# Attention and two mixture-of-experts layers in one kernel: small attention matmuls of two tiles in joined runs, weight splits on VectorE only, five residual-row buffers

## The chip, the cores and the metric

The kernel runs on one core of one Trainium2 chip. The metric is the device time of one execution in microseconds (us), as a median of several runs. The core has five engines with a queue of instructions each, which they work off in order: TensorE (PE, matmuls; its weight loads are listed apart as PEld), VectorE (DVE), ScalarE (ACT), GpSimd (POOL) and SyncE (SP, which here only issues DMAs). Engines wait for each other by semaphores.

## What is computed

```python
# q, k, v: (8, 8, 576, 64); attention inside chunks of 64 positions
scores = q_c @ k_c.T / sqrt(64); attn = softmax(scores); out = attn @ v_c
x = out.transpose(0, 2, 1, 3).reshape(4608, 512)
# layer 1, dense: w_in (512, 2048), w_out (2048, 512)
x = (s * relu(x @ w_in) ** 2 + b) @ w_out
# layer 2: 8 experts, w1[e] (512, 1024), w2[e] (1024, 512)
do = x @ w_skip > 0                       # other rows pass unchanged
e = argmax(x[do] @ w_gate); gate = softmax(x[do] @ w_gate)[e]
out[do] = x[do] + gate * (relu(x[do] @ w1[e]) @ w2[e])
```

All of it is float32. A product is made of three passes of a faster format: each operand is split into a high part (rounded) and a low part (the rest), and high x low, low x high and high x high are summed in PSUM.

## The kernel before

The 4608 rows are 36 tiles of 128 rows, in 13 chunks of 2, 3, 2, then nine times 3, then 2 tiles. Per tile `t` the attention is a chain over the engines: `att_sc` (TensorE, 16 matmuls of 64x64, line 230) writes the scores into PSUM, `att_max` and `att_sub` (VectorE), `att_exp` (ScalarE), `att_sum` (VectorE), `att_norm` (GpSimd or VectorE, line 255), `att_tr` (four transposes on TensorE, line 263), `att_cp` (ScalarE), `att_pv` (TensorE, 16 matmuls of 64x64, line 278), `att_hi` and `att_lo` (ScalarE, VectorE), which split the result into `xh` and `xl`. Queries and keys of one tile have one buffer (`qk`), the values one (`v`); the scores have the PSUM bank `sc`, the outputs `po`.

Per chunk `c` the dense layer takes 16 steps `f`: `p1_mm` (line 306, 12 matmuls into `ph`), `p1_sq` (ScalarE, lines 313 and 314) and `p1_g` (VectorE, lines 330 to 333), then `p2` (line 349, three matmuls per tile of the chunk into the `acc` banks). After step 15 `evac` (ScalarE, line 361) copies each tile's sum from PSUM into a residual-row buffer `x1` of the pool `op_`; from there it goes to `out` (line 364), its router logits are made (line 369 on VectorE, or lines 377 to 392 by way of TensorE), and after the routing (`route_a`, `route_b`, lines 409 to 462) the row, with its gate, is written to `x1s` in HBM (line 439). Only when that write has landed is the `x1` buffer free again. The pool has three such buffers. Chunk 1 accumulates in the banks `acc2`, `sc` and `tp`, so the scores of tile 7 need the copies of chunk 1 to be over. The last chunk copies two tiles. The weights of the dense layer are turned from int64 words into float32 and split in the first 130 us, and each conversion (`conv_scale`) holds an `x1` buffer too.

The second layer works on items: an expert's weights and up to 256 gathered rows. An item has 8 steps `mm1` (line 677, 12 matmuls) and 8 steps `mm2` (line 695, 6 matmuls). The expert's weights land as float32 in `whr` and `wlr` and are split into `win_h` (`split_hi`, ScalarE, line 636) and `win_l` (`split_lo`, line 639); step `f` of `mm1` needs split `f`, of `mm2` split `8 + f`. Items 0 and 1 are picked before the last chunk is routed; items 2 and on come from tables made of the counts (`tables_n`, `tables_b`, `table`), need the rows gathered by GpSimd (line 628), and run in a chain of branches at the end.

The order on all engines up to item 2 comes from `Plan`, a list scheduler in the kernel: `add` gives each operation its engine (or two to choose from), a cost, what it follows, an urgency, and rings of buffers that it takes and frees. `run` always puts the operation next that could start first, by those costs. So a changed ring or cost moves instructions everywhere.

Of the kernel before, what the change touches and what calls it, by code (L numbers as in the profile page):

```python
# [24 lines left out]
NTILE = NT // P  # L25
# [14 lines left out]
class Plan:  # L40
# [75 lines left out]
def fused_kernel(ctx: ExitStack, tc: tile.TileContext, qk, v, w_in, w_out, sb, wl, wlp, w1, w2,  # L116
# [6 lines left out]
    def pool(name, bufs=1, **kw):  # L123
        return ctx.enter_context(tc.tile_pool(name=name, bufs=bufs, **kw))
# [9 lines left out]
    ep = pool("ep", 2)  # L134
    qp = pool("qp")
    gp = pool("gp", 3)
    op_ = pool("op", 3)
    rp = pool("rp")
    ps = pool("ps", space=PSUM)
    ps_h = pool("ps_h", 2, space=PSUM)  # L140
# [148 lines left out]
    def att_hi(t):  # L289
        S.activation(out=xcols(t)[0], in_=po_t[t], func=AF.Copy)  # L290
# [63 lines left out]
    lg = {}  # L354
# [142 lines left out]
    r2 = {}  # L497
# [308 lines left out]
    with tc.manual_schedule():  # L806
# [29 lines left out]
                T.matmul(pro["pw"], zw[:, :P], zw, start=True, stop=True)  # L836

        rings = {n: 1 for n in ("acc0", "acc1", "acc2", "sc", "tp", "po", "qk", "v")}
        rings.update({"e": 2, "et": 2, "x1": 3, "ph": 2, "g": 3, "lg": 2, "xhl": 2, "r2": 3, "o": 2, "r": 2})
        fill(11)  # L840
        pl = Plan(rings, fill, "a0_0", {"DMA": 1.7, "PE": 5.8})
        add = pl.add
# [24 lines left out]
        def entry(t):  # L867
# [3 lines left out]
                return HURRY + t  # L871
            return 8 + 4 * (t - 5) if c == 2 else N0 + (c - 3) * NF + 5 * (t - T0[c])


        tags = {0: ("sc", "tp", "po"), 1: ("acc0", "acc1", "acc2"), 2: ("sc", "tp", "po"), 3: ("acc0", "acc1", "acc2"),
                4: ("sc", "tp", "po"), 5: ("po", "po", "po"), 6: ("po", "po", "po")}
# [4 lines left out]
            last[tag] = f"{done}{t}"  # L881
        for t in range(NTILE):
            for n in ("sc", "tr", "pv", "sub", "cp", "hi"):
                turn.setdefault(f"{n}{t}", []).extend([f"{n}{t - 1}"] if t else [])
        for t in range(NTILE):
            c = chunk_of[t]
            x, y, z = tags.get(t, ("sc", "tp", "po"))
            i = entry(t)
            h = i if t < 3 else i + HURRY / 2
            if t >= 5:  # L890
                add(f"ld_qk{t}", "DMA", 1.46, lambda t=t: load_qk(t), [f"ld_qk{t - 1 if t > 5 else 0}"], max(i - 8, 20 + 2 * (t - 5)), take=["qk"])
                add(f"ld_v{t}", "DMA", .73, lambda t=t: load_v(t), [f"ld_v{t - 1 if t > 5 else 0}"], max(i - 7, 21 + 2 * (t - 5)), take=["v"])
            w = [f"ev1_{j}" for j in range(3)] if t == 7 else []
            own = t == 0 or t >= 5
            add(f"sc{t}", "PE", 1.9 if t == 0 else 1.3, lambda t=t, x=x: att_sc(t, x), [f"ld_qk{t}"] + w + turn[f"sc{t}"], i,
                [x], [("qk", f"ld_qk{t}")] if own else [])
            add(f"mx{t}", "DVE", .6, lambda t=t: att_max(t), [f"sc{t}"], h)
            add(f"sub{t}", "DVE", .6, lambda t=t: att_sub(t), [f"mx{t}"] + turn[f"sub{t}"], h, ["e"], [(x, f"sc{t}")])
# [8 lines left out]
            add(f"pv{t}", "PE", 1.3, lambda t=t, z=z: att_pv(t, z), [f"cp{t}", f"ld_v{t}"] + turn[f"pv{t}"], i + 2, [z],  # L907
                [("et", f"cp{t}")] + ([("v", f"ld_v{t}")] if own else []))
            first = t == T0[c]
            add(f"hi{t}", "ACT", .48, lambda t=t: att_hi(t), [f"pv{t}"] + ([] if first else [f"hi{T0[c]}"]), h,  # L910
                ["xhl"] if first else [])
            add(f"lo{t}", "DVE", .6, lambda t=t: att_lo(t), [f"hi{t}"], h, [], [(z, f"pv{t}")])


        for u in range(2 * NF):
# [206 lines left out]
        for m in range(3):  # L1122
            i = iE + 20 * (m - 1)
            for u in range(16):
                if m == 0:
                    w = [f"a{L}_{u}"]
                else:
                    w = [f"m{m - 1}_{u}" if u < 8 else f"n{m - 1}_{u - 8}"]
                ld_ = f"s_w{m}{u // 8}" if m < 2 else f"t_w0{u // 8}"
                p = i + 4 + u  # L1130
                rw = (lambda m: r2["raw"][m % 2])
                add(f"sh{m}_{u}", "ACT", .52, lambda m=m, u=u: split_hi(r2["raw"][m % 2], u), [ld_] + w + ([f"sh{m}_{u - 1}"] if u else []), p)
                add(f"sl{m}_{u}", ("DVE", "POOL"), (.6, 1.23), lambda eng, m=m, u=u: split_lo(r2["raw"][m % 2], u, eng), [f"sh{m}_{u}"], p)
# [107 lines left out]
```

## Time and profile before

| | us |
|---|---|
| three runs | 1362.92, 1360.46, 1362.91; median 1362.91 |
| the profiled execution, its own time | 1361.95 |
| its span, first to last instruction | 1359.8 |
| PE busy in the span | 1301.1 (96%) |
| DVE busy | 987.0 (73%) |
| ACT busy | 571.7 (42%) |
| POOL busy | 199.5 (15%) |

All times in the rows are counted from the span's start. Matmul durations overlap: a 128x384 matmul is shown with 0.33 us and the next one starts 0.17 us later, so the distance of starts is what it costs. "x32" merges consecutive records; an instruction "x16" of the program shows as 32 records here. In brackets stands how long the engine had been idle and for whom it waited. Line numbers are those of the kernel before; up to line 836 the changed kernel has the same.

### The profile page before, as it was taken

The page shows a single profiled execution, that of the slowest core. Times are in us where ns is not written, and L with a number is a line of the kernel's source. Part 1 is how long each engine was busy: PE and PEld are TensorE (multiplying, and loading weights), DVE is VectorE, ACT ScalarE, POOL GpSimd, SP SyncE. Part 2 cuts the span into 40 slices and gives each one's busy share as a digit, 9 for nine tenths or more (in the row PEclk, how much of TensorE's full clock was granted, in tenths as well). Part 3 has the DMA queues.
Part 4 walks back from the last instruction along what each step waited for, and adds up shares of the span by engine and source line. Part 5 has one row for each costly group of instructions (what it writes and reads, how often), then busy time and mean ns, then how long its engine had stood idle before and what let it go on. Part 6 is the DMA issues. An engine that isn't in the chain of part 4 may idle for free. (4 is left out here: it accounts for less than half of the span.)

```text
span 1359.8 us, 23872 instructions
## 1 busy us (share of the span) xinstructions
PE 1301.1 (96%) x9107; PEld 1154.8 (85%) x9110; DVE 987.0 (73%) x2322; ACT 571.7 (42%) x1131; POOL 199.5 (15%) x210
## 2 busy tenths in 40 slices
PE   7899999999999999999999999999679999999896
PEld 5788888898888888888888888899668989999774
DVE  7896477649486775859486776847778888878674
ACT  4797433232232323232232333232526555656463
POOL 0000001000101010100101010101644212121243
PEclk9999989999999999999999999999889999999998
DMA  6553214111212132141213131112839656566473
GB/s 250 180 183 128 63 53 92 46 52 43 48 63 56 47 36 83 25 85 32 48 63 56 50 49 67 16 34 79 257 106 401 257 206 228 211 234 211 172 285 123
DMA packets 43019, 160.46 MB, mean 118 GB/s; under 512 B 11370, under 2 KB 11754, under 8 KB 38142
## 3 DMA queue, kind: packets, MB, share of 16 engines
q1 hardware_dynamic: 36526, 142.55, 33.6%
q0 software_dynamic: 6352, 16.12, 3.4%
q8 instruction: 78, 1.28, 0.4%
q14 instruction: 63, 0.52, 0.1%
HBM read 132.68 MB, written 27.20 MB: 118 GB/s over the span
## 5 line engine op out<-in xcount | busy, mean ns | idle before, releaser
L313 ACT ACTIVATE r<-ph 128x384 f32<-128x384 f32 (+1 forms) x208 | 96.5, 464 | 441.9 <-PE ph L306 433.0
L306 PE MATMUL ph<-xh,win_l 128*128 128x384 f32 (+1 forms) x832 | 274.9, 330 | 2.8 <-DVE win_l L206 1.4
L306 PE MATMUL ph<-xl,win_h 128*128 128x384 f32 (+1 forms) x832 | 269.6, 324 | 1.4 <-DVE xl L294 1.4
L306 PE MATMUL ph<-xh,win_h 128*128 128x384 f32 (+1 forms) x832 | 269.9, 324 | 0.0
L349 PE MATMUL acc<-wout_h,gl 128*128 128x512 f32 x544 | 220.4, 405 | 3.7 <-DVE gl L333 3.7
L349 PE MATMUL acc<-wout_l,gh 128*128 128x512 f32 x544 | 214.4, 394 | 0.0
L349 PE MATMUL acc<-wout_h,gh 128*128 128x512 f32 x544 | 213.0, 392 | 0.0
L330 DVE TENSOR_SCALAR r<-r,sb_sb 128x384 f32<-128x384 f32 (+1 forms) x176 | 84.8, 482 | 172.6 <-ACT r L314 166.9
L369 DVE CUSTOM_DVE_ANT_0 junk<-x,wl_sb 128x512 bf16<-128x512 f32 x270 | 191.3, 708 | 6.1 <-ACT x L361 0.4
L306 PEld LDWEIGHTS ph<-xh,win_l 128*128 128x128 f32 x832 | 156.5, 188 | 11.3 <-DVE win_l L206 2.1
L306 PEld LDWEIGHTS ph<-xl,win_h 128*128 128x128 f32 x832 | 156.6, 188 | 7.4 <-DVE xl L294 1.6
L695 PE MATMUL ac<-win_h,hhl 128*128 128x512 f32 x480 | 156.0, 398 | 1.1 <-DVE hhl L776 1.0
L306 PEld LDWEIGHTS ph<-xh,win_h 128*128 128x128 f32 x832 | 156.5, 188 | 0.0
L333 DVE TENSOR_TENSOR gl<-r,gh 128x384 fp32r<-128x384 f32 (+1 forms) x208 | 109.6, 527 | 30.2 <-ACT gh L320 24.1
L639 DVE TENSOR_TENSOR win_l<-wlr,win_h 128x512 fp32r<-128x512 f32 x121 | 98.4, 832 | 35.4 <-ACT win_h L636 35.3
L677 PE MATMUL ph<-xh,win_l 128*128 128x256 f32 x416 | 118.8, 286 | 3.8 <-ACT r L683 3.0
L349 PEld LDWEIGHTS acc<-wout_h,gh 128*128 128x128 f32 x544 | 102.4, 188 | 23.2
L349 PEld LDWEIGHTS acc<-wout_h,gl 128*128 128x128 f32 x544 | 102.5, 188 | 22.8 <-DVE gl L333 3.9
L677 PE MATMUL ph<-xl,win_h 128*128 128x256 f32 x416 | 118.3, 284 | 0.5 <-DVE xl L655 0.5
L677 PE MATMUL ph<-xh,win_h 128*128 128x256 f32 x416 | 118.2, 284 | 0.0
L349 PEld LDWEIGHTS acc<-wout_l,gh 128*128 128x128 f32 x544 | 102.8, 189 | 13.8
L695 PEld LDWEIGHTS ac<-win_h,hhl 128*128 128x128 f32 x480 | 91.4, 190 | 21.3 <-DVE hhl L776 2.7
(227 smaller groups left out, 2072.7 us busy)
## 6 DMA issues: line engine op xcount, KB each, us to landing
whr<-in_w SPq DMA_DIRECT2D x18, 2048.0 KB, 7.8
wlr<-in_w SPq DMA_DIRECT2D x18, 2048.0 KB, 10.8
qk<-in_qk SPq DMA_DIRECT2D x32, 512.0 KB, 10.0
x1s<-x SPq DMA_DIRECT2D x36, 264.0 KB, 9.1
out<-x SPq DMA_DIRECT2D x36, 256.0 KB, 2.3
v<-in_v SPq DMA_DIRECT2D x32, 256.0 KB, 2.7
stg<-in_w_in SPq DMA_DIRECT2D x16, 512.0 KB, 3.3
stg<-in_w_out SPq DMA_DIRECT2D x16, 512.0 KB, 3.3
```

The source lines that it names most:

```text
L306: T.matmul(ph, a[:, f, k * P:(k + 1) * P], b[c][:, k, :n], start=(i == 0), stop=(i == 11))
L313: S.activation(out=r, in_=ph_t.pop((c, f)), func=AF.Relu)
L330: V.tensor_scalar(out=r, in0=r, scalar1=sb_sb[:, 0:1], scalar2=sb_sb[:, 1:2], op0=ALU.mult, op1=ALU.add)
L333: V.tensor_tensor(out=gl, in0=r, in1=b32(gh), op=ALU.subtract)
L349: T.matmul(acc[c][j], a[:, j * P:(j + 1) * P], wo(b, f), start=(f == 0 and n == 0), stop=(f == NF - 1 and n == 2))
L369: V.tensor_tensor_reduce(out=junk, in0=x1t[T0[c] + j][:, :D], in1=wl_sb[0][:, i, :], op0=ALU.mult, op1=ALU.add, scale=1.0, scalar=0.0, acc ...
L639: ENG[eng].tensor_tensor(out=win_l[:, u, :], in0=raw[u // 8][:, u % 8, :], in1=b32(win_h)[:, u, :], op=ALU.subtract)
L677: T.matmul(ph, w[:, f, j * P:(j + 1) * P], r2[x][:, j, :], start=(n == 0), stop=(n == 11))
L695: T.matmul(ac[t], r2[h][:, f, t * P:(t + 1) * P], w[:, 8 + f, :], start=(f == 0 and n == 0), stop=(f == 7 and n == 2))
```

## The change

There are three edits.

The residual-row buffers `x1` go from three to five, in the pool and in the scheduler's ring.

For tiles 8 to 34 `att_pv(t)` and `att_sc(t + 1)` are one operation of the scheduler, `ps{t}`, so that the 64x64 matmuls of the two stand directly behind each other on TensorE. It follows all that the two followed. The scores of tile `t + 1` are so made earlier than before.

The splits `sl0`, `sl1` and `sl2` (the low parts of the weights of the items 0, 1 and 2) may no longer go to GpSimd.

```diff
-    op_ = pool("op", 3)
+    op_ = pool("op", 5)
...
-        rings.update({"e": 2, "et": 2, "x1": 3, "ph": 2, ...
+        rings.update({"e": 2, "et": 2, "x1": 5, "ph": 2, ...
...
+        JOIN = range(8, NTILE - 1)
+
+        def att_join(t):
+
+            att_pv(t, "po")
+            att_sc(t + 1, "sc")
...
+            if t - 1 not in JOIN:
+                add(f"sc{t}", "PE", 1.9 if t == 0 else 1.3, lambda t=t, x=x: att_sc(t, x), ...
...
+            if t in JOIN:
+                add(f"ps{t}", "PE", 2.2, lambda t=t: att_join(t),
+                    [f"cp{t}", f"ld_v{t}", f"ld_qk{t + 1}"] + turn[f"pv{t}"] + turn[f"sc{t + 1}"], i + 2, ["po", "sc"],
+                    [("et", f"cp{t}"), ("v", f"ld_v{t}"), ("qk", f"ld_qk{t + 1}")])
...
-                add(f"sl{m}_{u}", ("DVE", "POOL"), (.6, 1.23), lambda eng, m=m, u=u: split_lo(r2["raw"][m % 2], u, eng), [f"sh{m}_{u}"], p)
+                add(f"sl{m}_{u}", "DVE", .6, lambda m=m, u=u: split_lo(r2["raw"][m % 2], u, "DVE"), [f"sh{m}_{u}"], p)
```

What this does to the order shows at three places. The first is TensorE in a middle chunk, around the `att_pv` of one tile (`po`), first before:

```order
L306 MATMUL ph<-xl,win_h 128x384
L306 MATMUL ph<-xh,win_h 128x384
L278 MATMUL po<-et,v 64x64 x16
L349 MATMUL acc_3345<-wout_h_102,gl 128x512
L349 MATMUL acc_3345<-wout_l_103,gh 128x512
```

And now:

```order
L306 MATMUL ph<-xl,win_h 128x384
L306 MATMUL ph<-xh,win_h 128x384
L278 MATMUL po<-et,v 64x64 x16
L230 MATMUL sc<-qk 64x64 x16
L349 MATMUL acc_3345<-wout_h_102,gl 128x512
L349 MATMUL acc_3345<-wout_l_103,gh 128x512
```

The scores of the next tile, which stood by themselves some four large steps later, follow at once. In the order before, two of the 27 pairs already stood like this (tiles 8 and 9, and 9 and 10).

The second place is ScalarE at the end of chunk 1, whose three tiles are copied out of `acc`, `sc` and `tp`, first before:

```order
L313 ACTIVATE r<-ph 128x256
L314 ACTIVATE r<-r 128x256
L361 ACTIVATE x_1856<-acc_630 128x512
L313 ACTIVATE r<-ph 128x256
L314 ACTIVATE r<-r 128x256
L361 ACTIVATE x_1890<-sc 128x512
L361 ACTIVATE x_1897<-tp 128x512
```

And now:

```order
L313 ACTIVATE r<-ph 128x256
L314 ACTIVATE r<-r 128x256
L361 ACTIVATE x_1856<-acc_659 128x512
L361 ACTIVATE x_1858<-sc 128x512
L361 ACTIVATE x_1863<-tp 128x512
L313 ACTIVATE r<-ph 128x256
```

The three copies are made in a row. On TensorE the scores of tile 7 (`sc7`) move up one large step, to right behind the first `p2` of chunk 2.

The third place is VectorE after the last large step of the dense layer, from the split of item 0's rows (`xl`) on, first before:

```order
L655 TENSOR_TENSOR xl_9823<-tp2a,xh_9822 128x4x128
L655 TENSOR_TENSOR xl_9823<-tp2b,xh_9822 128x4x128
L639 TENSOR_TENSOR win_l<-whr_9810,win_h 128x512 x3
L688 CAST hhl<-r_9879 128x256
L689 TENSOR_TENSOR hhl<-r_9879,hhl 128x256
L392 COPY lg<-pl 128x9
```

And now:

```order
L655 TENSOR_TENSOR xl_9823<-tp2a,xh_9822 128x4x128
L655 TENSOR_TENSOR xl_9823<-tp2b,xh_9822 128x4x128
L392 COPY lg<-pl 128x9 x2
L409 TENSOR_REDUCE m<-lg 128x2
L410 TENSOR_TENSOR key<-lg,m 128x16
L411 TENSOR_TENSOR key<-key,cst_sb 128x16
```

The routing of the last chunk now stands ahead of item 0's splits; on TensorE its logits and counts likewise stand ahead of item 0's first `mm1`, where before they stood among its steps. And GpSimd, in the same stretch, had before:

```order
L639 TENSOR_TENSOR win_l<-whr_9810,win_h 128x512 x5
L436 MEMSET x_9863 128x15
L436 MEMSET x_9867 128x15
L639 TENSOR_TENSOR win_l<-wlr_9811,win_h 128x512 x2
L467 DMA idl<-ids_sb,si 37120x1 x2
L639 TENSOR_TENSOR win_l<-wlr_9811,win_h 128x512 x3
L639 TENSOR_TENSOR win_l<-whr_10055,win_h 128x512 x6
L708 DMA out<-et,idxs_9632 4608x512
```

And has now:

```order
L467 DMA idl<-ids_sb,si 37120x1 x2
L436 MEMSET x_9858 128x15
L436 MEMSET x_9860 128x15
L708 DMA out<-et,idxs_9632 4608x512 x2
L628 DMA xg_10264<-x1s,idx_9944 128x528 x2
```

24 splits of the items 0 to 2 leave GpSimd; VectorE has 48 of them instead of 24.

## Rows read from the trace of the kernel before

**Rows 1.** Waits of PE in the whole span: us in total, times, longest.
```profile
PE ac L695 <- DVE win_l L639: 8.3, 1, 8.3
PE tpl L377 <- ACT x L361: 7.5, 1, 7.5
PE sc L230 <- ACT x L361: 4.5, 1, 4.5
PE sc L230 <- DMA qk<-in_qk: 1.5, 1, 1.5
```

**Rows 2.** Windows: us, busy PE, PEld, DVE, ACT, POOL, clock, DMA share, GB/s.
```profile
165.09:954.32 789.23, 782.90 (x5671) 698.42 (x5669) 554.32 (x1500) 240.84 (x483) 73.51 (x98) 1.00 0.23 54
...
1041.52:1289.00 247.48, 244.87 (x1578) 223.70 (x1576) 201.32 (x386) 139.52 (x275) 47.61 (x42) 1.00 0.61 224
```

**Rows 3.** Timeline of PE around a lone `att_pv`: start us, us, instruction.
```profile
410.75 0.34 PE L306 MATMUL ph<-xh,win_h 128*128 128x384 f32 x1
411.02 1.15 PE L278 MATMUL po<-et,v 64*64 64x64 f32 x32
412.10 0.51 PE L349 MATMUL acc<-wout_h,gl 128*128 128x512 f32 x1
412.44 0.40 PE L349 MATMUL acc<-wout_l,gh 128*128 128x512 f32 x1
```

**Rows 4.** Timeline of PE where two runs already stood together, at two places.
```profile
26.89 2.08 PE L278 MATMUL po<-et,pro 64*64 64x64 f32 x64
...
212.62 0.84 PE L230 MATMUL sc<-qk 64*64 64x64 f32 x21 [0.30 <-issue]
```

**Rows 5.** DMA issues by line: KB each, median us from issue to landing.
```profile
qk<-in_qk SPq DMA_DIRECT2D x32, 512.0 KB, 10.0
```

**Rows 6.** Timeline of ACT at the second copy of chunk 1.
```profile
172.00 0.60 ACT L361 ACTIVATE x<-sc 128x512 f32<-128x512 f32 x1 [7.26 <-DMA x1s<-x]
```

**Rows 7.** Windows around the scores of tile 7.
```profile
168.14:172.65 4.51, 0.00 (x1) 0.00 (x1) 0.00 (x0) 0.65 (x2) 0.22 (x2) 0.80 0.12 12
172.65:178.84 6.19, 6.19 (x45) 5.20 (x45) 4.69 (x13) 2.45 (x6) 0.00 (x0) 0.60 0.49 172
```

**Rows 8.** Timeline of ACT at the first copy of the last chunk.
```profile
961.30 0.60 ACT L361 ACTIVATE x<-acc 128x512 f32<-128x512 f32 x1 [6.66 <-DMA x1s<-x]
```

**Rows 9.** Windows from the last `p2` to the first step of item 2.
```profile
954.32:962.72 8.40, 0.94 (x6) 0.77 (x5) 2.37 (x2) 1.62 (x4) 2.03 (x2) 0.80 0.72 120
962.72:978.31 15.59, 15.59 (x124) 15.50 (x123) 12.75 (x36) 10.77 (x24) 9.46 (x9) 0.89 0.99 390
978.31:1000.52 22.21, 13.91 (x51) 10.89 (x50) 21.31 (x56) 4.66 (x9) 12.10 (x10) 0.77 0.13 52
1000.52:1016.91 16.39, 13.09 (x105) 12.51 (x104) 12.27 (x28) 7.60 (x17) 9.82 (x9) 1.00 0.52 145
1016.91:1028.71 11.80, 11.80 (x58) 9.85 (x57) 6.34 (x7) 6.58 (x13) 4.80 (x4) 1.00 1.01 426
```

**Rows 10.** Timeline of DVE, two weight splits of item 0.
```profile
977.63 0.68 DVE L639 TENSOR_TENSOR win_l<-wlr,win_h 128x512 fp32r<-128x512 f32 x1
...
978.89 12.23 DVE L639 TENSOR_TENSOR win_l<-wlr,win_h 128x512 fp32r<-128x512 f32 x1
```

**Rows 11.** Timeline of POOL in the same stretch.
```profile
979.47 3.81 POOL L639 TENSOR_TENSOR win_l<-wlr,win_h 128x512 fp32r<-128x512 f32 x3
983.22 7.35 POOL L639 TENSOR_TENSOR win_l<-whr,win_h 128x512 fp32r<-128x512 f32 x6
```

**Rows 12.** Timeline of DVE in a chunk's routing, from its first to its last instructions.
```profile
943.28 0.17 DVE L409 TENSOR_REDUCE m<-lg 128x3 f32<-128x24 f32 x1
...
946.34 0.18 DVE L456 TENSOR_TENSOR sl<-pos,cst_sb 128x24 f32<-128x24 f32 x1 [0.40 <-PE pos L448]
...
947.15 0.56 DVE L462 TENSOR_TENSOR oacc<-oacc,ohb 128x8 bf16<-128x8 bf16 x3
```

**Rows 13.** Timeline of PE, the last chunk's logits among the steps of item 0.
```profile
967.64 1.85 PE L388 MATMUL pl<-wlt,et 128*128 128x9 f32 x16
```

More of the change, by code (lines that the diff above doesn't have):

```diff
@@ L838, in fused_kernel @@
         rings = {n: 1 for n in ("acc0", "acc1", "acc2", "sc", "tp", "po", "qk", "v")}
-        rings.update({"e": 2, "et": 2, "x1": 3, "ph": 2, "g": 3, "lg": 2, "xhl": 2, "r2": 3, "o": 2, "r": 2})
+        rings.update({"e": 2, "et": 2, "x1": 5, "ph": 2, "g": 3, "lg": 2, "xhl": 2, "r2": 3, "o": 2, "r": 2})
         fill(11)
@@ L872, in entry, with home @@
             return 8 + 4 * (t - 5) if c == 2 else N0 + (c - 3) * NF + 5 * (t - T0[c])
+        def home(n, t):
+            if n == "sc" and t - 1 in JOIN:
+                return f"ps{t - 1}"
+            return f"ps{t}" if n == "pv" and t in JOIN else f"{n}{t}"
+        JOIN = range(8, NTILE - 1)
+        def att_join(t):
+            att_pv(t, "po")
+            att_sc(t + 1, "sc")
         tags = {0: ("sc", "tp", "po"), 1: ("acc0", "acc1", "acc2"), 2: ("sc", "tp", "po"), 3: ("acc0", "acc1", "acc2"),
@@ L883, in fused_kernel @@
             for n in ("sc", "tr", "pv", "sub", "cp", "hi"):
-                turn.setdefault(f"{n}{t}", []).extend([f"{n}{t - 1}"] if t else [])
+                turn.setdefault(f"{n}{t}", []).extend([home(n, t - 1)] if t else [])
         for t in range(NTILE):
@@ L894, in fused_kernel @@
             own = t == 0 or t >= 5
[L895 to L898, printed above, removed]
+            if t - 1 not in JOIN:
+                add(f"sc{t}", "PE", 1.9 if t == 0 else 1.3, lambda t=t, x=x: att_sc(t, x), [f"ld_qk{t}"] + w + turn[f"sc{t}"], i,
+                    [x], [("qk", f"ld_qk{t}")] if own else [])
+            add(f"mx{t}", "DVE", .6, lambda t=t: att_max(t), [home("sc", t)], h)
+            add(f"sub{t}", "DVE", .6, lambda t=t: att_sub(t), [f"mx{t}"] + turn[f"sub{t}"], h, ["e"], [(x, home("sc", t))])
             add(f"ex{t}", "ACT", .52, lambda t=t: att_exp(t), [f"sub{t}"], h)
@@ L906, in fused_kernel @@
             add(f"cp{t}", "ACT", .48, lambda t=t: att_cp(t), [f"tr{t}"] + turn[f"cp{t}"], h, ["et"], [(y, f"tr{t}")])
-            add(f"pv{t}", "PE", 1.3, lambda t=t, z=z: att_pv(t, z), [f"cp{t}", f"ld_v{t}"] + turn[f"pv{t}"], i + 2, [z],
-                [("et", f"cp{t}")] + ([("v", f"ld_v{t}")] if own else []))
+            if t in JOIN:
+                add(f"ps{t}", "PE", 2.2, lambda t=t: att_join(t),
+                    [f"cp{t}", f"ld_v{t}", f"ld_qk{t + 1}"] + turn[f"pv{t}"] + turn[f"sc{t + 1}"], i + 2, ["po", "sc"],
+                    [("et", f"cp{t}"), ("v", f"ld_v{t}"), ("qk", f"ld_qk{t + 1}")])
+            else:
+                add(f"pv{t}", "PE", 1.3, lambda t=t, z=z: att_pv(t, z), [f"cp{t}", f"ld_v{t}"] + turn[f"pv{t}"], i + 2, [z],
+                    [("et", f"cp{t}")] + ([("v", f"ld_v{t}")] if own else []))
             first = t == T0[c]
-            add(f"hi{t}", "ACT", .48, lambda t=t: att_hi(t), [f"pv{t}"] + ([] if first else [f"hi{T0[c]}"]), h,
+            add(f"hi{t}", "ACT", .48, lambda t=t: att_hi(t), [home("pv", t)] + ([] if first else [f"hi{T0[c]}"]), h,
                 ["xhl"] if first else [])
-            add(f"lo{t}", "DVE", .6, lambda t=t: att_lo(t), [f"hi{t}"], h, [], [(z, f"pv{t}")])
+            add(f"lo{t}", "DVE", .6, lambda t=t: att_lo(t), [f"hi{t}"], h, [], [(z, home("pv", t))])
         for u in range(2 * NF):
```

## The prediction

> **What bounds the kernel now.** I read the page's table of engines first: PE is busy 96% of the span, so the time is TensorE's work plus what it waits. Then the windows [rows 2]. From 165.09 to 954.32 PE is busy 782.90 of 789.23 us at a clock of 1.00, and from 1041.52 on it is busy 244.87 of 247.48. In those stretches only less TensorE work, or cheaper changes between kinds of it, makes the kernel shorter, and whatever is saved ahead of 1041 moves all that follows forward by the same amount. Third the list of PE's waits [rows 1]: four of them are large, 8.3, 7.5, 4.5 and 1.5 us, and they lie at two places, the end of chunk 1 (4.5) and the stretch between the last `p2` and item 2 (7.5 and 8.3). The 1.5 us wait is for a load of queries and keys.
>
> **Part A, five residual-row buffers.** The wait of 4.5 us is that of the scores of tile 7, which need chunk 1 copied out of `sc`. That copy itself had stood 7.26 us for the write of a chunk 0 row to `x1s` [rows 6]: with three buffers, the rows of chunk 1 can only go where rows of chunk 0 have left. With five, two rows of chunk 0 and three of chunk 1 fit, so no copy of chunk 1 waits for a write, and the new order has the three copies in a row. That takes the idle window of 4.51 us away [rows 7]. Behind it stands a second cost: the granted clock was 0.60 in the 6.19 us after the wait, a mix of the two levels 1.2 and 2.4 GHz, with PE busy throughout. At the full level that work takes about 6.19 × 0.60 = 3.7 us, or 2.5 less; matmuls of 64x64 lose less by the clock than large ones, so I take 2.2. Gain 4.5 + 2.2 = 6.7 us; bounds 4.5 (the clock falls anyway, for another short wait) and 7.0. Next in line behind the copies are the softmax of tile 7 and its transposes, which in the new order have as many large steps between them as before, so I see nothing late there.
>
> **Part B, joined runs.** A lone `att_pv` costs [rows 3]: it starts 0.27 us after the matmul ahead of it instead of 0.17, so 0.10 to enter; 412.10 − 411.02 = 1.08 for the run; then 0.34 to the second 128x512 matmul, where 0.17 × 512/384 = 0.23 is the usual distance, so 0.11 to leave. That is 1.29 us, and 2.58 for `att_pv` and `att_sc` apart. Joined, the trace shows 64 records in 2.08 us without a gap [rows 4], the last of them shown with its own depth; the second run then costs 0.98 instead of 1.29. Gain 0.31 per pair. Of 27 pairs two stood together already: 25 × 0.31 = 7.7 us, taken as 7.6. The bounds are 0 and 7.7: in one place where the two already stood together, the second run stopped 0.30 us for "issue" [rows 4], and such a stop in every joined run would eat the gain. I stay near the upper end, because that is the one stop of its kind among the 64x64 runs from 165 to 954.
>
> The join adds a wait. The second half needs the queries and keys of tile `t + 1`; their buffer is free only when the scores of tile `t` are done, which is the end of the joined run before. A median load takes 10.0 us from issue to landing [rows 5]. By the order, two joined runs mostly stand two or more pairs of large steps apart, about 24 us of TensorE work; only those of tiles 9 and 10, around the end of a chunk, stand some 11 us apart. Behind a late load the rest of TensorE's queue would stand, and with it `p1` and `p2`. I take 0.5 us of loss for the close pair, bounds 0 and 3. The 1.5 us wait that is there already [rows 1] stays.
>
> **Part C, from the last `p2` to item 2.** Before, this takes 1028.71 − 954.32 = 74.39 us, in five windows [rows 9] with PE busy 0.94 + 15.59 + 13.91 + 13.09 + 11.80 = 55.3 and idle 19.06.
>
> The largest wait, 8.30 us in the third window, is for a split of item 0's second weights. VectorE makes such a split in 0.68 us, but the one that began at 978.89 took 12.23 [rows 10]. GpSimd meanwhile made nine splits without a pause, from 979.47 to 990.57 [rows 11], and VectorE's ended when that run did. Without splits on GpSimd I expect 0.68 there, and the wait gone. After the wait the clock was at the lower level; the window's 0.77 over 22.21 us is 5.1 us lost, some of it under the wait. I take 2.8 as lost by work; bounds 0 and 5.1.
>
> By the Trainium skill ("SBUF — State Buffer", section "Who interferes with whom") a VectorE instruction with two SBUF inputs contends with GpSimd's reads, and the one that issues first holds the shared ports for the whole instruction. By that rule alone one split of GpSimd, about 1.3 us in rows 11, would hold VectorE, not nine in a row; the trace shows 12.23. Rival 2 below is what that would mean.
>
> What takes the place: VectorE makes 24 more splits, 24 × 0.68 = 16.3 us [rows 10]. By the order 17 of them belong to items 0 and 1. In the second to fourth windows VectorE shows 12.75 + 21.31 + 12.27 = 46.3 us [rows 9], of which 12.23 − 0.68 = 11.6 were the stand; in exchange come 17 × 0.68 = 11.6, so 46.3 again. By my sum items 0 and 1 take TensorE from 962.3 to 1012.6, 50 us. So VectorE is close behind, but not the bound if the two run side by side.
>
> The first window, 8.40 us, I leave as it is. Before, the copies of the last chunk waited 6.66 us for `x1s` writes [rows 8], and five buffers end that; but in the new order the routing of the last chunk stands ahead of item 0's splits on VectorE, which works in order, and the first `mm1` needs a split. The chain is two copies (2 × 0.60), their transposes and logits, the two routing parts (from 943.28 to 947.71 in a chunk of three, 4.43 us with other work between; without it about 3) [rows 12], and a split of 0.68. From 954.3 that comes to about 962.0, at worst 963.5. The wait of 7.5 us for the copies becomes one of like length for a split, and the clock loss behind it (0.89 in the second window) stays. But the transposes, logits and counts of the last chunk, which stood among the steps of item 0 (the logits alone 1.7 us [rows 13], with the rest about 2.6), now fall under this wait.
>
> The fourth window has 16.39 − 13.09 = 3.30 us of waits, behind the stall on the engines that feed `mm1` of item 1. I take 1.9 as gone, bounds 0 and 3.3. Sum of part C: 8.3 + 2.8 + 2.6 + 1.9 + 0.4 (962.3 in place of 962.72) = 16 us; 58 of the 74.4 us are left. The weights of item 2, issued when its buffer comes free, then land some 4 us before they are needed by the 10 us of a landing, so they do not decide, though not by much.
>
> **Other edits.** In the first 130 us the conversions take more buffers and change order; the windows there are not TensorE-bound everywhere. I take 0, bounds −1.5 and +1.5.
>
> **Sum.** 6.7 + 7.6 − 0.5 + 16 = 29.8, about 30 us, from the profiled execution's 1361.95: 1332. The median of the runs is 0.96 above that execution, so I predict **1333 us**.
>
> **Rivals.**
> 1. *The joined runs gain nothing* (each has the 0.30 stop of rows 4, or waits as long for its load). The trace has one such stop in some 55 runs, which speaks against it. 1333 + 7.6 = about 1340. Chance 0.12.
> 2. *The 12.23 us were not GpSimd's splits.* If VectorE stood for something else, 8.3 + 2.8 stay: 1344. That it ended with GpSimd's run speaks against it. Chance 0.06.
> 3. *VectorE becomes the bound of items 0 and 1.* The 16.3 us that it gets then come onto the path, part C gains nothing, and the time is 1333 + 16 = 1349. For it: 46 beside 50 us is close, and the routing goes first. Against it: in the second window PE was busy all 15.59 us beside 12.75 of VectorE [rows 9]. Chance 0.10.
> 4. *The change does not do what it says* (pairs not joined, splits still shared). The order excludes it for TensorE and GpSimd; that the run differs from its order I give 0.01.
> 5. *Slower: the joined runs starve.* The second half stands for the load of `qk`, which SP issues in order behind row writes. To cost the 30 us won it must cost 30/25 = 1.2 us in each pair, that is, landings of 24 + 1.2 = about 25 us against the median 10.0 [rows 5]. From landings of 24 us on it begins, at 25.2 the kernel is no faster, and at 27 it is 45 us worse off than forecast, 1378. The 1.5 us wait [rows 1] is the only trace of it. Chance 0.03.
>
> **How the numbers follow.** My forecast has the remaining chance of 0.68. Its own range is that of its bounds: clocks (−2 to +3), fourth window and the start of item 0 (−1.4 to +3), prologue (±1.5), joins (0 to +3), which together give 1327 to 1339. The range reaches down to 1325 and up through rivals 1 and 2, to 1346: outside are rival 3, in part, rival 5, and a rest. About 0.2% (2.7 us) is what a measurement of this kernel can tell from no change. All but rival 5 and part of 4 are faster by more: faster 0.95, same 0.02, slower 0.03.
>
> **What would show it right or wrong.** In the profile after, PE's waits of rows 1 for a copy in `att_sc` and for a split in `mm2` should be gone; that in front of item 0 stays at about 7.5 us, with a split or its like as releaser. Each `po` run should be followed by an `sc` run 0.98 us later with no idle time between (rival 1: 0.30 of "issue", or waits for `qk`; rival 5: the same waits of a microsecond and more). No split should stand on GpSimd before item 2, and those of VectorE should take 0.68 (rival 2: one of many microseconds is left). The window from the last `p2` to item 2 should be about 58 us (rival 3: 74, with VectorE busy throughout). The prediction is wrong if PE is not TensorE-bound between 165 and the last `p2`, or if a new wait for weights stands in front of item 2.

## The result and the profile after

The changed kernel takes 1345.4 us (median of 1343.9 to 1346.2) where the kernel before took 1362.8 on the same chip: a ratio of 0.9875, with a 95% interval of 0.9858 to 0.9892. The gain is 17.4 us. The forecast was 30 us, 1333, with 1327 to 1339 as its own range, which the time misses. It lies inside the stated range, 1325 to 1346, only because that had been stretched upward for rivals 1 and 2, and neither of them came: the sign was right, the size was not.

The profiled execution takes 1345.51 us with a span of 1343.6, 16.2 less than before. Where that comes from is read from the starts of the same matmul in both traces: the last `p2` of a chunk, the first `mm1` or `mm2` of an item, the last matmul. The last column is the same kernel traced again on another chip (run a_same below), against the same trace of before.

| stretch | before, us | after, us | gain | forecast | gain, traced again |
|---|---|---|---|---|---|
| start to the last `p2` of chunk 1 | 162.03 | 164.02 | -2.0 | 0 | -3.6 |
| chunk 2 | 64.10 | 57.32 | 6.8 | 6.7 | 6.6 |
| chunks 3 to 12 | 728.0 | 720.6 | 7.3 | 7.1 | 7.4 |
| last `p2` to `mm2` of item 1 | 62.8 | 55.0 | 7.9 | 16 | 13.9 |
| `mm2` of item 1 to the branches | 273.4 | 272.3 | 1.0 | 0 | 0.1 |
| branches to the last matmul | 61.2 | 63.8 | -2.6 | 0 | -3.7 |
| last matmul to the end of the span | 8.4 | 10.6 | -2.2 | 0 | -2.4 |

(The `mm2` of item 1, 11.8 us in all three traces, lies in the fifth row; the 16 us were forecast for the stretch that ends behind it.) First PE's waits in the whole span, as in [rows 1]: us in total, times, longest.

```profile
PE ph L763 <- issue: 6.1, 2, 4.8
PE acc L349 <- DVE gl L333: 5.5, 8, 1.8
PE ph L677 <- ACT r L683: 5.4, 2, 4.3
...
PE pos L445 <- DVE ohb L416: 1.7, 1, 1.7
PE sc L230 <- DMA qk<-in_qk: 1.5, 1, 1.5
```

The 8.3, 7.5 and 4.5 us of [rows 1] are gone; the 1.5 us for queries and keys stayed. New are 4.3 us (of the 5.4) for ScalarE in item 1, and more waits for `gl` (8 instead of 4).

At the end of chunk 1 the three copies now stand in a row on ScalarE without a wait, where the second had stood 7.26 us [rows 6]:

```profile
163.13 0.58 ACT L361 ACTIVATE x<-acc 128x512 f32<-128x512 f32 x1
163.76 0.60 ACT L361 ACTIVATE x<-sc 128x512 f32<-128x512 f32 x1
164.45 0.60 ACT L361 ACTIVATE x<-tp 128x512 f32<-128x512 f32 x1
```

The joined runs look as the prediction wanted them; this is the place of [rows 3] on PE, and the second run starts 0.98 us after the first and ends into the next large matmul:

```profile
403.61 0.34 PE L306 MATMUL ph<-xh,win_h 128*128 128x384 f32 x1
403.88 1.15 PE L278 MATMUL po<-et,v 64*64 64x64 f32 x32
404.86 1.10 PE L230 MATMUL sc<-qk 64*64 64x64 f32 x32
405.89 0.51 PE L349 MATMUL acc<-wout_h,gl 128*128 128x512 f32 x1
```

And the stretch from the last `p2` to item 2, with the columns of [rows 2], against [rows 9] (which begin 0.23 us later, at the end of the last `p2` instead of its start, and part the third window from the fourth at the transposes of item 1's rows, where these have its first `mm1`):

```profile
941.96:949.63 7.67, 4.21 (x33) 3.06 (x31) 3.66 (x21) 6.53 (x13) 1.64 (x2) 0.73 0.64 48
949.63:965.20 15.57, 14.50 (x97) 14.30 (x97) 10.61 (x26) 4.94 (x12) 2.48 (x4) 0.81 1.03 307
965.20:977.89 12.69, 11.95 (x59) 9.77 (x57) 11.86 (x56) 7.50 (x16) 0.48 (x1) 1.00 0.60 244
977.89:996.92 19.03, 13.87 (x97) 13.27 (x97) 11.63 (x30) 6.68 (x15) 7.59 (x8) 0.91 0.74 242
996.92:1008.73 11.81, 11.81 (x59) 9.85 (x58) 11.42 (x20) 9.38 (x18) 0.00 (x0) 1.00 1.01 434
```

The third and fourth window once more, parted where [rows 9] part them:

```profile
965.20:976.11 10.91, 10.91 (x50) 8.96 (x49) 10.11 (x52) 6.36 (x13) 0.00 (x0) 1.00 0.68 284
976.11:996.92 20.81, 14.91 (x106) 14.07 (x104) 13.38 (x35) 7.82 (x17) 8.07 (x8) 0.92 0.68 221
```

The third window lost 11.3 us of its 22.21: the stand of VectorE is gone. The second kept its length (15.57 for 15.59), though the last chunk's logits had left it, and the fourth grew from 16.39 to 20.81.

### The profile page after: what moved, and what is told of

It is laid out like the page before. It is cut to its first block, busy times and chain, and to the rows that moved or that the text cites. A ratio compares the mean times of both kernels' runs of the same rounds, so it can differ in the third digit from the quotient of the medians.

```text
span 1343.6 us, 23837 instructions
## 1 busy us (share of the span) xinstructions
PE 1294.0 (96%) x9110; PEld 1154.1 (86%) x9110; DVE 964.9 (72%) x2346; ACT 575.3 (43%) x1131; POOL 164.8 (12%) x186
## 5 line engine op out<-in xcount | busy, mean ns | idle before, releaser
L369 DVE CUSTOM_DVE_ANT_0 junk<-x,wl_sb 128x512 bf16<-128x512 f32 x270 | 185.8, 688 | 5.7
L639 DVE TENSOR_TENSOR win_l<-wlr,win_h 128x512 fp32r<-128x512 f32 x130 | 90.1, 712 | 41.1 <-ACT win_h L636 41.1
```

Of the source, the lines that this page charges most:

```text
L369: V.tensor_tensor_reduce(out=junk, in0=x1t[T0[c] + j][:, :D], in1=wl_sb[0][:, i, :], op0=ALU.mult, op1=ALU.add, scale=1.0, scalar=0.0, acc ...
L639: ENG[eng].tensor_tensor(out=win_l[:, u, :], in0=raw[u // 8][:, u % 8, :], in1=b32(win_h)[:, u, :], op=ALU.subtract)
```

## The experiments

Each is timed beside the kernel before, in the same study on the same chip; its median there was 1367.2 us in the first study, 1361.8 in the second, 1366.0 in the third and 1367.2 in the last. Ratios compare best across studies. The kernel before was traced on the first chip alone, so the stretches of all runs are set against that one trace. Long lines of a diff are shown in part.

| run | what | us | ratio, 95% interval |
|---|---|---|---|
| e_x1 | before + five buffers | 1361.2 | 0.9955 (0.9938 to 0.9972) |
| e_join | before + joined runs | 1359.9 | 0.9939 (0.9922 to 0.9955) |
| e_split | before + splits on VectorE | 1360.3 | 0.9951 (0.9934 to 0.9968) |
| a_nosplit | after, splits shared again | 1361.6 | 0.9953 (0.9932 to 0.9973) |
| a_same | after | 1343.0 | 0.9867 (0.9850 to 0.9883) |
| a_nojoin | after without the joins | 1346.3 | 0.9899 (0.9875 to 0.9923) |
| a_late | after, item 2's gathers later | 1343.5 | 0.9868 (0.9852 to 0.9885) |
| a_early | after, item 0 earlier | 1345.8 | 0.9888 (0.9872 to 0.9905) |
| e_gap | before, memsets between GpSimd's splits | 1369.1 | 1.0019 (1.0006 to 1.0031) |
| a_fix | after, conversions in three buffers, memsets | 1347.1 | 0.9860 (0.9837 to 0.9883) |
| a_best | after, three edits | 1344.3 | 0.9826 (0.9800 to 0.9853) |
| a_best3 | a_best and one more | 1342.2 | 0.9806 (0.9788 to 0.9824) |

### The parts alone

e_x1:

```diff
-    op_ = pool("op", 3)
+    op_ = pool("op", 5)
...
-"x1": 3
+"x1": 5
```

> The kernel before with five residual-row buffers alone. My theory: in the trace of the changed kernel the end of chunk 1 gave 6.8 us and the stretch ahead of it lost 2.0; both come with the buffers. GpSimd keeps its splits (ten in a row by the order), so VectorE stands beside them for about 10 us again and the stretch from the last p2 to item 2 gains nothing: 1362.8 - 6.8 + 2.0 = 1358 (1355 to 1361). Rival, the buffers' new order is what ends the long stand, not the splits: that stretch gains the 7.6 us that the changed kernel shows there, 1350.

Measured 0.9955, that is 6 us. In the trace chunk 2 takes 58.16 us instead of 64.10, and chunk 1 74.89 instead of 72.47 (72.81 and 72.51 in e_join and e_split, with three buffers on this chip): the gain and the loss both come with the buffers, as expected. The stretch from the last `p2` to item 2 did not stay as it was, though: it takes 68.57 us instead of 74.62, most of what the rival said. The long stand of VectorE did not come back: GpSimd has a run of six splits here too, but VectorE's instructions got through beside it, one at a time, each as long as one split of GpSimd. VectorE and GpSimd in that stretch:

```profile
974.36 1.27 DVE L579 TENSOR_SCALAR tuo<-ca,cst_sb 128x16 f32<-128x16 f32 x1
975.66 1.21 DVE L580 SCALAR_TENSOR_TENSOR tuo<-stt,cst_sb,tuo 128x16 f32<-128x16 f32 x1
976.90 1.21 DVE L581 CUSTOM_DVE_ANT_0 tujk<-tuo,bs 128x16 f32<-128x16 f32 x1
...
994.93 3.17 DVE L639 TENSOR_TENSOR win_l<-wlr,win_h 128x512 fp32r<-128x512 f32 x1 [0.24 <-ACT win_h L636]
```
```profile
971.41 7.91 POOL L639 TENSOR_TENSOR win_l<-wlr,win_h 128x512 fp32r<-128x512 f32 x6 [6.78 <-ACT win_h L636]
...
994.98 2.56 POOL L639 TENSOR_TENSOR win_l<-wlr,win_h 128x512 fp32r<-128x512 f32 x2
```

The three small instructions take 1.2 us each; the kernel before runs the same three, free of GpSimd, in 0.17 to 0.23. The last split of VectorE, begun 0.05 us ahead of two of GpSimd, waits out both: 3.17 us. In item 2 splits of both engines stand beside each other once more:

```profile
1016.74 6.48 DVE L639 TENSOR_TENSOR win_l<-whr,win_h 128x512 fp32r<-128x512 f32 x4 [5.34 <-ACT win_h L636]
```
```profile
1016.27 6.41 POOL L639 TENSOR_TENSOR win_l<-whr,win_h 128x512 fp32r<-128x512 f32 x4 [10.73 <-ACT win_h L636]
```

These four of VectorE are as large as the one that took 12.23 us, and began inside GpSimd's run: each took 1.4 to 1.8 us. From `mm2` of item 1 to the branches this run takes 5.2 us more than the kernel before, and from there to the last matmul 3.5 more, so the time gains less than the stretches ahead.

e_join takes the rest of the change's diff, with three buffers and shared splits:

```diff
+        JOIN = range(8, NTILE - 1)
...
+            if t in JOIN:
+                add(f"ps{t}", "PE", 2.2, lambda t=t: att_join(t),
```

> The kernel before with the joined runs alone. My theory: 25 new pairs give 0.3 each, 7.3 us as between chunk 2 and chunk 11 of the changed kernel, and nothing else moves: 1355.5 (1354 to 1357). Rival, the joins only gain where the buffers let the loads run ahead: under 4 us, 1359 to 1363.

Measured 0.9939, 8 us, with an interval from 6 to 11. The trace shows more of it than the time. Every middle chunk with three pairs goes from between 76.03 and 76.09 us to between 75.02 and 75.17: about 0.33 us per pair. Chunk 6 alone goes the other way, from 76.03 to 79.60, for two stops inside one joined run and a clock of 0.57 in the 4 us behind them:

```profile
511.63 0.39 PE L230 MATMUL sc<-qk 64*64 64x64 f32 x6
512.57 0.93 PE L230 MATMUL sc<-qk 64*64 64x64 f32 x24 [0.55 <-issue]
515.50 0.35 PE L230 MATMUL sc<-qk 64*64 64x64 f32 x2 [2.01 <-issue]
```

The changed kernel has the same stop in the same chunk, of 0.81 us, which leaves that chunk without a gain (76.15 for 76.03):

```profile
505.55 0.42 PE L230 MATMUL sc<-qk 64*64 64x64 f32 x6 [0.81 <-issue]
```

What lies around it: from 504.5 to 507.0 the DMA queues of that trace show a packet of each of the two instruction queues, of which the packets of q8 otherwise come 10 to 25 us apart:

```profile
q1 hardware_dynamic: 126, 0.23, 41.9%
q8 instruction: 1, 0.02, 2.4%
q14 instruction: 1, 0.01, 1.3%
```

In every trace that has the stop a packet of q8 starts within 0.5 us after it (505.9 here, 515.6 in e_join). So the stop comes together with a load of instructions, in a run whose records follow each other every 0.03 us, where large matmuls take 0.17 to 0.23. But that load begins when the stop is over, so it is not what ended it. The stop is 0.8 to 0.9 us in the first profile and the second study, 2.0 to 2.8 in the other studies. That TensorE waits there for instructions is a reading that is not shown: no experiment of its own forced it, and why it happens at this one pair is open.

e_split:

```diff
-                add(f"sl{m}_{u}", ("DVE", "POOL"), (.6, 1.23), lambda eng, m=m, u=u: split_lo(r2["raw"][m % 2], u, eng), [f"sh{m}_{u}"], p)
+                add(f"sl{m}_{u}", "DVE", .6, lambda m=m, u=u: split_lo(r2["raw"][m % 2], u, "DVE"), [f"sh{m}_{u}"], p)
```

> The kernel before with the splits of items 0 to 2 on VectorE only. My theory: the wait of 8.3 us in item 0's second product and the low clock behind it go, some 9.5 us; the first window after the last p2 stays at 8.4 since copies still wait for buffers: 1353 (1350 to 1356). Rival, VectorE becomes the bound of items 0 and 1 by its 16 us more: 1360 or over, with VectorE busy without a pause there.

Measured 0.9951, 7 us. The wait of 8.3 us for a split is gone, and the stretch from the start of the last `p2` to item 2 takes 65.63 us instead of 74.62, 9.0 less: the size expected. PE's waits there are these two, and VectorE is busy 49.08 of the 65.63, so it does not become the bound (rival 3). One thing was expected otherwise: item 0 begins 0.99 us behind the last `p2`, and the wait of 6.5 us for the copies falls inside its first product. 5.4 us are given back at the end of the program (below).

```profile
PE tpl L377 <- ACT x L361: 6.5, 1, 6.5
PE ph L677 <- DVE win_l L639: 4.3, 2, 3.7
```

a_nosplit is the changed kernel with the first line of that diff in place of the second.

> The changed kernel with the splits of items 0 to 2 shared with GpSimd again. My theory: VectorE stands for some 10 us beside ten splits of GpSimd in a row, and the 8.9 us that the changed kernel gained from the last p2 to item 2 go: 1345.4 + 8.9 = 1354 (1351 to 1357). Rival, the long stand belonged to something else in the old order: within 2 us of the changed kernel, 1344 to 1347.

Measured 0.9953 against 0.9875 and 0.9867 of the changed kernel: 11 us of its 18 go. The expected size was 9; the mechanism was not the expected one long stand, but many short ones as in e_x1. Where the loss lies, the two traces of the changed kernel leave open in part: the stretch from the last `p2` to item 2 takes 70.97 us, 4.2 more than in after and 10.2 more than in a_same, and the one from there to the branches 6.4 and 5.5 more. 3.5 us more are lost in chunk 6, by a stop of 2.83 us in the joined run, and 2.2 are won at the end. So the split edit may be worth more beside the others (11 us, 5 to 17 by the ends of the intervals) than alone (7), but the intervals do not show it.

### The rest of the missing gain

a_same is the changed kernel, unchanged.

> The changed kernel again, as the one to compare with on this chip. My theory: the parts of the first study that gained less than forecast did so by waits that change from chip to chip (instruction loads inside the joined runs, row writes), so the ratio to the kernel before stays near 0.9875 and the time is 1345 to 1351 on a chip where the kernel before takes 1363 to 1367. Rival, the gain was that of one chip: 1355 or more.

0.9867: the gain is not that of one chip. But its trace differs in one stretch. Windows of a_same, the same as the third to fifth of after:

```profile
967.37:980.05 12.68, 11.94 (x58) 9.76 (x56) 11.85 (x56) 7.49 (x16) 0.55 (x1) 1.00 0.52 210
980.05:992.71 12.66, 11.89 (x97) 11.69 (x98) 11.79 (x30) 6.71 (x15) 7.53 (x8) 1.00 0.63 174
992.71:1004.51 11.80, 11.80 (x58) 9.85 (x57) 9.03 (x16) 5.74 (x11) 0.00 (x0) 1.00 1.01 415
```

Item 1's `mm1` takes 12.66 us here and 19.03 in the first trace, with the same instructions in the same order. Parted as in [rows 9], the fourth window takes 14.43 us here, 2.0 less than before. In the first trace ScalarE took up a finished step about 5 us late, TensorE then waited for ScalarE, and went on at the lower clock (0.91 over the window):

```profile
989.57 0.41 PE L677 MATMUL ph<-xh,win_l 128*128 128x256 f32 x1 [4.30 <-ACT r L683]
```
```profile
989.13 0.66 ACT L683 ACTIVATE r<-ph 128x256 f32<-128x256 f32 x2 [5.09 <-remote]
```

The last matmul of the step that ScalarE takes at 989.13 had started on TensorE at 983.21. GpSimd issues six gathers in a row meanwhile, which led to the next run.

a_late:

```diff
-("tu", 0, ["t_u", "m0_0"])
+("tu", 0, ["t_u", "m1_7"])
...
-["t_d_tu0"] + [f"sl0_{8 * which + u}" for u in range(8)]
+["t_u"] + [f"sl0_{8 * which + u}" for u in range(8)]
```

> The changed kernel with the gathers for the items from 2 on made after item 1's first product instead of during it, and item 2's weights no longer issued behind their landing. Theory G: while GpSimd issues the six gathers in a row, what TensorE reports as done reaches the other engines late, and item 1's first product stands 4.3 us for it; with the gathers elsewhere that wait goes, and the clock does not fall behind it: 5 us faster than the changed kernel beside it, unless item 2's rows then come late. Rival, the stand belongs to that place for another reason (an instruction load, a split): a wait of 2 us or more stays in item 1's first product.

Measured the same as a_same (0.9868), and `mm1` of item 1 takes 12.33 us. Since a_same has no stand there either, with the gathers in the old place, theory G is not borne out: the gathers alone do not make the stand. What makes it in some executions stays open. The kernel before has a smaller one of 1.9 us in item 1's first product, which I had counted as going; in a_same and a_late it went.

a_nojoin:

```diff
-        JOIN = range(8, NTILE - 1)
+        JOIN = range(0)
```

> The changed kernel without the joined runs (five buffers and the splits stay). My theory: 0.3 us for each of 25 pairs, less what instruction loads stop in joined runs: 4 to 7 us slower than the changed kernel beside it, and no stop for issue over 0.4 us at a run of 64x64 matmuls. Rival, the joins give nothing in the changed kernel: within 1 us of it.

0.9899 against 0.9867: about 4 us slower, at the lower edge of what was expected, with intervals that overlap. Its trace is clearer: the chunks take 76.01 to 76.07 us again, chunk 6 too, and no stop for "issue" stands at a 64x64 run behind chunk 1. Something else shows in it: item 0's second weights land in time, no split on ScalarE stands for them, and item 0's `mm1` takes 13.57 us, where it takes 15.57 in after and 16.07 in a_same, whose splits stood 2.00 and 2.60 us for that load. The stretch from the last `p2` to item 2 takes 57.95 us, the 58 of the forecast.

a_early:

```diff
-add(f"s_w0{which}", "DMA", 5.9 + 2 * (1 - which),
+add(f"s_w0{which}", "DMA", 1.0 + 2 * (1 - which),
...
-[f"b{L}_7", "s_2", f"s_d{which}"] + (["s_w00"] if which else []), iL + 10)
+[f"b{L}_7", "s_2"] + (["s_w00"] if which else ["s_d0"]), iL + 10)
```

> The changed kernel with the scheduler told that item 0's first weights are there early, as the trace shows them, and with its second weights issued without a wait for item 1's rows. My theory: item 0's splits then stand ahead of the last chunk's routing, and the window of 7.67 us between the last p2 and item 0 shrinks to under 2 us, with the low clock behind it gone: 6 to 8 us faster than the changed kernel, if the second weights land in time, 2 to 4 if they do not. Rival, the window is kept by something else (the copies, the banks): same as the changed kernel within 1.5 us.

The window in front of item 0 shrinks from 7.67 to 2.37 us, and nothing is gained: 0.9888. The first two windows, last `p2` to item 0 and item 0's `mm1`:

```profile
942.88:945.25 2.37, 1.72 (x10) 0.84 (x8) 1.10 (x3) 2.28 (x5) 1.01 (x1) 1.00 0.54 8
945.25:968.25 23.00, 16.13 (x118) 15.79 (x119) 12.02 (x41) 11.12 (x25) 2.39 (x4) 0.85 0.93 334
```

TensorE stands 6.86 us for ScalarE in that product. On ScalarE the reason is plain: a split of the second weights stands 8.07 us for their load, and the `r` that TensorE waits for is queued behind it.

```profile
957.93 1.67 ACT L636 ACTIVATE win_h<-wlr 128x512 fp32r<-128x512 f32 x3 [8.07 <-DMA wlr<-in_w]
959.50 0.36 ACT L683 ACTIVATE r<-ph 128x256 f32<-128x256 f32 x1
```

So the wait in front of item 0, which the prediction left as it was, covers a later one for the second weights.

### What holds VectorE

e_gap:

```diff
+    def split_gap(raw, u, eng):
+        split_lo(raw, u, eng)
+        if eng == "POOL":
+            G.memset(gap, 0.0)
```

> The kernel before with one more GpSimd instruction, the memset of a 128x1 tile, behind each of its 24 splits; the order is otherwise as before. Theory H: VectorE's split loses to GpSimd only because one split of GpSimd follows the other at once, so an instruction between them that reads nothing lets VectorE through: the stand of 12.23 us beside nine splits becomes 1.3 to 3 us, TensorE's wait of 8.3 us in item 0's second product goes for the most part, and the kernel is 5 to 8 us faster than the kernel before. Rival, a split of VectorE stands until GpSimd has nothing more to do: again 11 to 14 us and the time of the kernel before, within 2 us.

Theory H falls: VectorE's split took 12.54 us beside nine splits with memsets between them, against 12.23 without [rows 10].

```profile
983.81 12.54 DVE L639 TENSOR_TENSOR win_l<-wlr,win_h 128x512 fp32r<-128x512 f32 x1
```
```profile
984.39 1.34 POOL L639 TENSOR_TENSOR win_l<-wlr,win_h 128x512 fp32r<-128x512 f32 x1
985.62 0.14 POOL L646 MEMSET gap<- 128x1 f32 x1
...
994.49 1.30 POOL L639 TENSOR_TENSOR win_l<-whr,win_h 128x512 fp32r<-128x512 f32 x1
```

VectorE's began first, 0.58 us ahead of GpSimd's first, and ended 0.56 us after the last. By the Trainium skill ("SBUF — State Buffer", section "Who interferes with whom") a VectorE instruction with two SBUF inputs contends with GpSimd's reads, and whoever issues first holds the shared ports for the whole instruction. That the two contend, these traces show; that the first holds the ports, they do not. In the five traces with splits on both engines (before, e_x1, e_join, a_nosplit, e_gap) ten splits of VectorE between the last `p2` and the branches began 0.05 to 0.6 us ahead of a run of GpSimd's, and each ended 0.55 or 0.56 us after that run, however long: 2.26 us beside one, 3.17 beside two, 4.70 beside three, 12.23 to 12.54 beside nine. VectorE's splits that began inside a run took 1.4 to 1.8 us each, as the four in item 2 of e_x1. So of two instructions of the same shape it is the one that began first that waits for the whole run; why is open.

### Chunk 1, the end, and a faster version

a_fix:

```diff
-[f"st{u}"] + ([f"ca{u - 1}"] if u else []), i, ["x1"])
+[f"st{u}"] + ([f"ca{u - 1}"] if u else []) + ([f"cl{u - 3}"] if u > 2 else []), i, ["x1"])
...
+        split_lo(raw, u, "DVE")
+        if u % 2:
+            G.memset(gap, 0.0)
```

(The memsets come behind every second split of the items 0 to 2, 24 in all.)

> The changed kernel with two edits that lie far apart in time: the conversions of the dense weights keep at most three of the five buffers, and GpSimd gets 24 memsets of a 128x1 tile, about as many instructions as the splits that it lost. My theory on the first: the 2.3 us that chunk 1 takes longer with five buffers come from conversions running ahead on VectorE and ScalarE, and chunk 1 is back from 74.2 or more to 72.5 us; rival, they come from the copies in a row, and it stays. My theory on the second: the 2.2 us that lie more between the last matmul and the end of the span (10.5 against 8.3) hang on where GpSimd's instructions fall into the blocks in which they are loaded, and change; rival, they come from the last rows' write, and stay at 10.5. Together 1340 to 1343 where the changed kernel takes 1343 to 1345.

The first edit does what was expected: chunk 1 takes 72.52 us, as before (72.47), instead of 74.21. The waits in chunk 1, of after and then of a_fix:

```profile
PE acc L349 <- DVE gl L333: 1.7, 4, 0.8
```
```profile
PE acc L349 <- DVE gl L333: 0.4, 1, 0.4
```

(Before, it is one wait of 0.3 us.) a_best and a_best3, which have this edit without the memsets, show 72.51 and 72.58 us for chunk 1. So the 1.7 us more come from the conversions that five buffers let run ahead on VectorE and ScalarE. The time as a whole, 0.9860, is not to be told from a_same: chunk 2 waits 2.0 us for a load of values on this chip, and chunk 6 stops 2.2 us for "issue".

On the second edit: the last stretch takes 9.5 us here, 10.6 in the changed kernel and 8.4 before. In that stretch the queue q14 loads three blocks of instructions in the kernel before and four in the changed one, and also in e_gap, whose only difference to the kernel before is 24 memsets on GpSimd and whose last stretch is 10.7 us:

```profile
q14 instruction: 3, 0.02, 0.9%
```
```profile
q14 instruction: 4, 0.03, 1.0%
```

(the first of before, the second alike in after and e_gap). The span ends 4.3 to 4.6 us after the start of the last of these loads in before, after and a_fix alike. So the 2.2 us come with a block more to load. The four traces in which GpSimd has its 24 splits and nothing more (before, e_x1, e_join, a_nosplit) all have three blocks and 8.4 us there; the other ten have four, and 9.5 to 10.7. a_fix itself has four: with 24 memsets for the 24 splits the number of instructions is about as before and the block does not go, so that the number alone decides is not shown.

The 2.6 to 3.7 us more between the branches and the last matmul may be of the same kind: the waits of PE that grow there have "issue" as their releaser (4.9 us once before, 4.8 and 1.3 after). e_join and e_gap, with GpSimd's splits and three buffers, lose at most 0.2 there, but e_x1 loses 3.5 and e_split 3.1. So the five buffers alone bring this loss, and the split edit alone does; what the two have in common was not tried.

a_best has the first edit of a_fix and those of a_early, and issues item 0's second weights right behind the first (against the line of a_early):

```diff
-(["s_w00"] if which else ["s_d0"]), iL + 10)
+(["s_w00"] if which else ["s_d0"]), iL + 10 - 100 * which)
```

> The changed kernel with the conversions held to three buffers, item 0's weights known to be early, and its second weights issued right behind the first. In the study before, item 0 began 6 us earlier and then stood 6.9 us behind the second weights, whose load had been queued behind row writes. My theory: that load, issued 11 us earlier, ends the stand, item 0's second product begins 13 us after its first and item 2 some 6 to 9 us earlier than in the changed kernel; with chunk 1's 2.3 us, 1334 to 1338. Rival, the transfers share the same engines, so the first weights, the row writes or item 1's weights come later by as much: 1341 or more.

The stand behind the second weights is gone: item 0's `mm2` begins 13.9 us after its `mm1`, and item 1 begins 28.6 us after the last `p2` (35.9 in after). But item 1's `mm1` then waits 5.7 us for its splits, since VectorE makes the tables of the items ahead of them, and chunk 12 is 1.9 us longer, by a wait for gathered rows that was not there. The ratio is 0.9826, a smaller gain than forecast.

a_best3 moves one table:

```diff
-        add("t_h", "DVE", 1.9, table_h, ["t_u"], i - 8)
+        add("t_h", "DVE", 1.9, table_h, ["t_u", "sl1_3"], i - 8)
```

> The version before this one (conversions held to three buffers, item 0's weights early) with one more edit: the second table of the items, 1.9 us on VectorE, is made after the first four splits of item 1 instead of ahead of them, since item 1's first product stood 5.7 us for those splits. My theory: about 2.5 of the 5.7 us go, and less of the low clock follows: a ratio of 0.981 to the kernel before, 1336 to 1340 where that takes 1362. Rival, the splits then wait for something else (their weights, ScalarE's halves): the ratio stays at 0.9826, or rises.

0.9806, interval 0.9788 to 0.9824: it lies below both ratios of the changed kernel (0.9875 and 0.9867) and their intervals. Its item 0 runs as it should, 13.65 and 11.87 us at full clock; item 1's `mm1` still takes 19.07, with 4.7 us of waits for splits, where 2.5 of the 5.7 us were expected to go. Its interval overlaps that of a_best, so what the last edit gives is not shown.

```profile
945.32:947.70 2.38, 1.71 (x10) 0.84 (x8) 1.11 (x3) 2.29 (x5) 0.00 (x0) 1.00 0.72 53
947.70:961.35 13.65, 13.65 (x118) 13.56 (x119) 11.85 (x41) 10.71 (x24) 1.80 (x2) 1.00 1.00 291
961.35:973.22 11.87, 11.87 (x59) 9.92 (x58) 10.72 (x43) 7.47 (x15) 0.53 (x3) 1.00 0.71 193
973.22:992.29 19.07, 13.74 (x98) 13.15 (x96) 14.48 (x48) 4.90 (x12) 6.02 (x6) 0.91 0.58 195
```

## Why the prediction was right, and where it was not

**Part A was right.** 6.7 us forecast, 6.8 measured in chunk 2, and e_x1 shows that the buffers alone do it. Both terms held: the wait went, and the clock did not fall behind it (1.00 over the 57.32 us of chunk 2).

**Part B was right in mechanism and size.** 0.31 us per pair forecast, about 0.33 measured; 7.1 us net forecast, 7.3 measured. The loss was put in the wrong place: I took 0.5 us for a late load of `qk` between close pairs, which did not come, and held the stop for "issue" of [rows 4] to be the one of its kind. In the joined runs it comes once, with 0.8 us, and on other chips with 2 and more. Rival 1 was a matter of one pair, not of all.

**Part C failed in size: 16 us forecast, 7.9 and 13.9 in two traces.** By its terms, each in the windows of [rows 9]:
- The 8.3 us wait and the 2.8 us of low clock behind it: the window went from 22.21 to 10.91, 11.3 for 11.1, in both traces. GpSimd's splits were the cause (e_split, a_nosplit; shared in another order, in e_x1, they leave a wait of 3.7 us); rival 2 falls.
- The 2.6 us of logits and counts that leave item 0's `mm1`: nothing (15.57 and 16.07 for 15.59). This work now runs ahead of the wait, as said, but ScalarE then stands 2.0 and 2.6 us for item 0's second weights, by which a step of TensorE waits 1.1 and 1.7 us, and the clock stays low for longer (0.81 and 0.82 for 0.89). Where those weights came in time (a_nojoin), 2.0 us were won. The prediction had not asked when they land, and had left the clock of that window as it was.
- The 1.9 us of the fourth window: 2.0 in a_same, and a loss of 4.4 in the first trace, for the wait of 4.3 us for ScalarE and the low clock behind it (0.92). Here I had called a wait gone whose cause I did not know; that it went in a_same, and came back longer in the first trace, is luck on either side.
- The first window of 8.4, left as it is: right (7.67), and for the reason given. That nothing could be won there without the second weights, which a_early showed, the prediction did not see.

**What was not in the sum at all** costs nearly as much as the miss of part C in the first trace, and more in the second: the end of the program (-4.8 and -6.1 us) and chunk 1 (-2.0 and -3.6). For the conversions I had allowed 1.5 us either way, taken at 0, with no wait of chunk 1 read for it; a_fix shows that it is VectorE's `gl`, late behind the conversions. For the end there was no term, because no edit touches it; the runs show that two of the three edits lengthen it, and not by what.

**Two sums were wrong.** The bounds given for the forecast's own range add up to 1328 to 1344, not to 1327 to 1339; the time misses that too. And in rival 5, landings of 27 us would cost 3 us in each of 25 pairs, 75 in all: 1408, not 1378. Neither changes the forecast.

**Rivals 3 and 5** did not come: VectorE is busy 49.18 of the 66.77 us from the last `p2` to item 2, and the one wait for `qk` in the dense layer is the old one of 1.5 us.

## What to carry to other kernels

A wait that is taken away gives its length only up to the next late thing on the same path: ask for each engine that feeds the place which load or which split comes last when everything is earlier, as with the second weights behind item 0. More buffers also let unrelated work run ahead on the shared engines; bound that where the other work is urgent (three buffers for the conversions, five for the rows). Elementwise work split over VectorE and GpSimd can be slower than on VectorE alone (e_split), so price it in the trace, not by the sum of their rates.

## What was not expected of the hardware

- A VectorE split that began just ahead of a run of GpSimd splits stood until the run ended (12.23 and 12.54 us beside nine, 4.70 beside three, 3.17 beside two), also with a 0.1 us memset between them, while VectorE's instructions begun inside a run passed one by one at 1.2 to 1.8 us.
- 24 harmless GpSimd instructions more (e_gap) or 24 fewer (after) both lengthened the last 8.4 us of the program, by 2.3 and 2.2, with one block of instructions more loaded there.
- A joined run of 64x64 matmuls stopped 0.8 to 2.8 us for "issue" at one and the same place of the program, beside a load of instructions.
- Two executions of the same program differ by 6.4 us in one item's first product (19.03 and 12.66), with no difference in order; the cause stays open.
